# A sixth token group with 16 instead of 12 row pairs in seven products, and LN2 transposes that wait for both tiles' stores

## The chip, the cores and the metric

One core of one Trainium2 chip. The metric is the time of one execution on the device, in microseconds (us), as the median of several executions. Engines: PE is TensorE, ACT is ScalarE, DVE is VectorE, POOL is GpSimd, SP is SyncE, which issues nearly all DMAs. LN2 is the layer norm ahead of the MLP.

## The reference, cut to what matters

```
h  = x + A(layernorm(x))                 # sliding, dilated attention, S = 2048, D = 576, 32 heads; ends in @ wo
h2 = h + gelu(layernorm(h) @ w1 + b1) @ w2 + b2        # F = 4608
```

## The kernel before

Tokens are worked in 8 groups of two tiles of 128. Each group goes through MLP1 (324 matmuls), and then through MLP2, in the middle of which stands Wo, the attention's output product, for the *next* group. MLP2 sums over F = 36 blocks of 128, taken as 18 row pairs. A pair is a 2x2 block product and may be done with 7 matmuls (products P1 to P7) in place of 8, if DVE first makes sums of the h blocks and of the w2 blocks. From the third group on some of the 18 pairs are done so: 8, 12, 12, 12, 18 and 18.

The order of one MLP2 with 12 pairs, and what its words do (cut):

```
ROWS = {2: 8, 3: 12, 4: 12, 5: 12, 6: NM, 7: NM}                  # k = 5 is the sixth group; NM = 18
steps = [(1, all_), "b", "wo", "h", "e", (2, all_), "11", (6, all_), "d", "6", "7", (7, all_), "rest", "in",
         (5, all_), "f", "exp", (4, all_), "21", "22", "o1", "4", (3, all_), "12", "o0", "3"]
# (n, rows): product n on PE.   "11" "12" "21" "22": the rows that are left plain, on PE.
# "b", "d", "f": ACT copies one PSUM bank into another, which the next product adds to:
seed = {"b": (1, 6), "d": (6, 5), "f": (5, 3)}                    # "d" copies P6's bank into P5's
nc.scalar.copy(out=bank[seed[step][1]], in_=bank[seed[step][0]])
# "h": LN2's statistics and the last sums;  "6", "7": ACT scales tile c, tile d, and SP stores them;
# "in": the two DMA transposes of these stores, which the next MLP1 reads (hnT)
...
def dma_out(src):                                                 # a tile is stored by two DMAs, 144 KB and 16 KB
    td = dram.tile([P, KT * P], BF16, tag="td", name="td", bufs=4)
    nc.sync.dma_start(out=td[:, 0:D], in_=src)
    nc.sync.dma_start(out=td[:, D:KT * P], in_=src[:, KF * P:D])
    return td

def ln2_in(j):
    read[0] = nc.sync.dma_start_transpose(out=hnT_slot(j), in_=hn.pop(j)[:]).ins
```

The instructions of an engine run in the order in which this code issues them. In what follows c and d are the first and the second tile of the next group.

## Time and profile before

| | before |
|---|---|
| time, median (lowest to highest) | 365.13 (364.87 to 365.61), 3 runs |
| PE busy, matmuls | 359.0 us of 363.3, 4899 |
| sixth group, first MLP2 matmul to the next group's first MLP1 matmul | 272.10 to 290.79 = 18.69 us |

The last row is the piece that the change is about. It is read from the timeline of PE, and it has 168 matmuls and no gap. The lines behind these numbers are in the prediction; one more on which it rests is c's second store of the sixth group's input, held up while an instruction fetch was under way:

```profile
246.03 1.92 SPq L192 DMA_DIRECT2D td<-hn  x1
```

### The profile page before, as it was taken

The page shows a single profiled execution, that of the slowest core. Times are in us where ns is not written, and L with a number is a line of the kernel's source. Part 1 is how long each engine was busy: PE and PEld are TensorE (multiplying, and loading weights), DVE is VectorE, ACT ScalarE, POOL GpSimd, SP SyncE. Part 2 cuts the span into 40 slices and gives each one's busy share as a digit, 9 for nine tenths or more (in the row PEclk, how much of TensorE's full clock was granted, in tenths as well). Part 3 has the DMA queues.
Part 4 walks back from the last instruction along what each step waited for, and adds up shares of the span by engine and source line. Part 5 has one row for each costly group of instructions (what it writes and reads, how often), then busy time and mean ns, then how long its engine had stood idle before and what let it go on. Part 6 is the DMA issues. An engine that isn't in the chain of part 4 may idle for free.

```text
span 363.3 us, 11427 instructions
## 1 busy us (share of the span) xinstructions
PE 359.0 (99%) x4899; PEld 292.3 (80%) x4899; DVE 299.1 (82%) x422; ACT 229.3 (63%) x507; POOL 39.4 (11%) x47
## 2 busy tenths in 40 slices
PE   8999999999999999999999999999999999999996
PEld 5688977888788877887788778877987788778874
DVE  5999999999899999999999899979994599720431
ACT  4779856799527763668456855685568556615630
POOL 2251004000120030103100211020101010100000
PEclk9999999999999999999999999999999999999999
DMA  7979999965455833711652156304530442030001
GB/s 235 321 187 294 231 261 233 366 217 80 144 101 96 194 134 87 153 39 35 143 99 71 35 134 108 70 32 106 121 70 33 90 86 56 3 90 18 2 2 33
DMA packets 61907, 43.70 MB, mean 120 GB/s; under 512 B 31888, under 2 KB 60176, under 8 KB 61856
## 3 DMA queue, kind: packets, MB, share of 16 engines
q1 hardware_dynamic: 59968, 41.13, 43.2%
q0 software_dynamic: 1728, 1.77, 4.6%
q8 instruction: 38, 0.62, 0.7%
q10 hardware_dynamic: 160, 0.07, 0.1%
q14 instruction: 13, 0.11, 0.1%
HBM read 21.10 MB, written 12.42 MB: 92 GB/s over the span
## 4 chain that ended last, share of the span: by engine, by line
PE 98%; DMA 1%; DVE 0%; ACT 0%; SPq 0%; issue 0%
PE pm L215 39%; PE po L659 27%; PE pq L215 15%; PE po L574 10%; PE pw L215 5%; PE xt_pt L182 1%; DMA x_all<-in_A_x_dram 1%; PE xt_pt L186 0%; ACT q_all L810 0%; PE h_pt L182 0%; PE o_pt L182 0%; DVE o_sb L690 0%; SPq L104 0%; DVE q_all L789 0%; PE h_pt L186 0%; PE o_pt L186 0%
## 5 line engine op out<-in xcount | busy, mean ns | idle before, releaser
L555 ACT ACTIVATE h_all<-pm,b_sb 128x256 f16<-128x256 f32 (+1 forms) x288 | 108.5, 497 | 76.7 <-PE pm L215 76.7
L215 PE MATMUL pm<-hnT,w_sb 64*128 64x256 bf16 x2304 | 143.0, 269 | 0.0
L215 PEld LDWEIGHTS <-w_sb 64*128 64x128 bf16 x2304 | 112.0, 94 | 14.7 <-issue 1.7
L659 PEld LDWEIGHTS <-h_all 128*128 128x128 f16 x544 | 52.3, 98 | 15.3 <-issue 2.5
L215 PE MATMUL pq<-wq_sb,xnT 64*128 64x288 bf16 x768 | 54.4, 283 | 0.0
L215 PEld LDWEIGHTS <-xnT 64*128 64x128 bf16 x864 | 42.8, 94 | 9.8 <-DMA xnT<-xd 0.2
L349 DVE TENSOR_TENSOR prod<-prod 128x2304 bf16<-128x2304 bf16 (+1 forms) x64 | 44.2, 691 | 2.1
L659 PE MATMUL po<-w2a_sb,h_all 128*128 128x288 bf16 (+1 forms) x312 | 43.6, 286 | 0.0
L395 DVE TENSOR_TENSOR prod<-kv_ring,probs 128x4608 bf16<-128x4608 bf16 x16 | 40.9, 2555 | 0.4
L343 DVE TENSOR_TENSOR prod<-kv_ring,q_all 128x4608 bf16<-128x4608 bf16 x16 | 40.8, 2549 | 0.2
L215 PE MATMUL pm<-hnT,w1h_sb 64*128 64x256 bf16 x288 | 39.3, 269 | 0.0
L401 DVE TENSOR_TENSOR prod<-prod 128x2304 bf16<-128x2304 bf16 (+1 forms) x32 | 33.8, 1057 | 1.0
L574 PEld LDWEIGHTS <-h_all 128*128 128x128 bf16 x288 | 27.9, 98 | 7.9 <-issue 0.9
L479 POOL TENSOR_TENSOR ln_rstd<-ln_var,mhalf 128x1 f32<-128x1 f32 x13 | 14.4, 1108 | 174.7 <-ACT ln_var L478 174.7
L574 PE MATMUL po<-w2a_sb,h_all 128*128 128x288 bf16 x224 | 28.5, 286 | 0.0
L659 PEld LDWEIGHTS <-kv_ring 128*128 128x128 f16 x240 | 23.5, 98 | 5.9
L659 PE MATMUL po<-w2b_sb,h_all 128*128 128x288 bf16 (+1 forms) x152 | 22.2, 286 | 0.0
L639 DVE TENSOR_TENSOR kv_ring<-h_all 128x1536 f16<-128x1536 f16 (+3 forms) x10 | 6.9, 686 | 16.0 <-ACT h_all L555 16.0
L215 PE MATMUL pw<-wo_sb,oT 64*128 64x288 bf16 x256 | 19.5, 283 | 0.0
L162 POOL TENSOR_TENSOR ln_rstd<-ln_veps,mhalf 128x1 f32<-128x1 f32 (+2 forms) x14 | 13.4, 962 | 47.9 <-DVE ln_veps L156 31.6
L215 PEld LDWEIGHTS <-oT 64*128 64x128 bf16 x288 | 13.5, 94 | 4.8 <-issue 1.7
L503 POOL DMA_DIRECT2D x_all<-h x12 | 10.9, 1060 | 54.6 <-DMA x_all<-in_A_x_dram 25.0
(107 smaller groups left out, 375.9 us busy)
## 6 DMA issues: line engine op xcount, KB each, us to landing
w_sb<-in_B_w_dram SPq DMA_DIRECT2D x6, 768.0 KB, 6.1
kv_ring<-kv_dram SPq DMA_DIRECT2D x28, 144.0 KB, 2.7
w2a_sb<-in_B_w_dram SPq DMA_DIRECT2D x4, 1008.0 KB, 6.3
kv_dram<-kv_ring SPq DMA_DIRECT2D x13, 288.0 KB, 4.6
out_dram<-o_sb SPq DMA_DIRECT2D x15, 144.0 KB, 2.7
td<-q_all SPq DMA_DIRECT2D x14, 144.0 KB, 2.5
td<-hn SPq DMA_DIRECT2D x14, 144.0 KB, 1.8
x_all<-in_A_x_dram SPq DMA_DIRECT2D x12, 144.0 KB, 3.0
```

What stands on the lines that cost most here:

```text
L162: nc.gpsimd.tensor_tensor(out=rstd[:], in0=veps[:], in1=mhalf[:].to_broadcast([P, n]), op=ALU.pow)
L215: last = nc.tensor.matmul(duo["g"][r ^ swap][i], lhsT=lhsT, rhs=rhs, start=(swap == 0 and i == 0 and kt == 0), stop=(swap == 1 and kt == K ...
L343: nc.vector.tensor_tensor(out=prod[:], in0=k_ring[j % 2], in1=q_all[:, j, :].unsqueeze(1) .to_broadcast([P, W, D]), op=ALU.mult)
L349: nc.vector.tensor_tensor(out=prod[:, :, o * H:o * H + n], in0=prod[:, :, a * H:a * H + n], in1=prod[:, :, c * H:c * H + n], op=ALU.add)
L395: nc.vector.tensor_tensor(out=prod[:].rearrange("p w (d h) -> p w d h", h=H), in0=v_ring[j % 2].rearrange("p w (d h) -> p w d h", h=H), in ...
L401: nc.vector.tensor_tensor(out=prod[:, 0:n, :], in0=prod[:, 0:n, :], in1=prod[:, n:2 * n, :], op=ALU.add)
L479: nc.gpsimd.tensor_tensor(out=rstd[:], in0=var[:], in1=mhalf[:], op=ALU.pow)
L503: ins = nc.gpsimd.dma_start(out=x_of(j), in_=h_of.pop(j)[:], accum_op=ALU.add).ins
L555: pace[0] = nc.scalar.activation(out=hT(grp)[:, f, 0:N], in_=ps[:, r, i * N:(i + 1) * N], func=ACT.Gelu_apprx_tanh, bias=b1_sb[:, f:f + 1] ...
L574: nc.tensor.matmul(banks[half], lhsT=hT(grp)[:, f, i * P:(i + 1) * P], rhs=w2_rows(f)[:, half * HALF:(half + 1) * HALF], start=(f == 0), s ...
L639: nc.vector.tensor_tensor(out=s_slot(t, m0, m1), in0=a, in1=b, op=alu)
L659: nc.tensor.matmul(bank, lhsT=l, rhs=r, start=start, stop=stop, skip_group_check=True)
```

## The change

Four row pairs more of the sixth group go through the seven products: four matmuls fewer. The sums for them come late on DVE, so the first 12 rows of P6 and P7 go ahead of the last 4 of each. Besides, at every group the first LN2 transpose waits until tile d's last store has landed, so that no LN2 store is in flight beside an LN2 transpose. Cut to its core:

```diff
     def dma_out(src):
...
-        nc.sync.dma_start(out=td[:, D:KT * P], in_=src[:, KF * P:D])
+        stored[0] = nc.sync.dma_start(out=td[:, D:KT * P], in_=src[:, KF * P:D]).ins
...
     def ln2_in(j):
         read[0] = nc.sync.dma_start_transpose(out=hnT_slot(j), in_=hn.pop(j)[:]).ins
+        if stored[0] is not None:
+            tc.add_manual_dep(read[0], stored[0].name, sync_dep, reason="stores ahead of the transposes of LN2")
+            stored[0] = None
...
+        if SR < rows < NM:                                        # SR = 12
+            steps = [(1, all_), "b", "wo", "h", "e", (2, all_), "11", (6, lo), (7, lo), "6", "7", (6, hi), "d", (7, hi), "rest", "in",
+                     (5, all_), "f", "exp", (4, all_), "21", "22", "o1", "4", (3, all_), "12", "o0", "3"]
...
-        ROWS = {2: 8, 3: 12, 4: 12, 5: 12, 6: NM, 7: NM}
+        ROWS = {2: 8, 3: 12, 4: 12, 5: 16, 6: NM, 7: NM}
...
+                if k == 5:
+                    m1[1] += [c_(w2_sums, 12, 14)]
+                    x["h"] += [c_(h_sums, SR, rows), c_(w2_sums, 14, 16)]
...
-                    m1[1] = [c_(w2_sums, *m) for m in ((12, 14), (14, 16), (16, NM))]
+                    ring1_free[0] = True
+                    m1[1] = [c_(w2_sums, 16, NM)]
```

(Cut: the rows of q_all in which the new sums and "rest" are kept, and that only the first 12 rows' sums are called where all were.)

More of the change, by code (lines that the diff above doesn't have):

```diff
@@ L186, in transpose_in @@
         nc.tensor.transpose(pt[0:HP, KF, :], src[:, KF * P:D], ident[:])
+    stored = [None]
     def dma_out(src):
@@ L609 @@
     SR = 12
+    ring1_free = [False]
     RING_T = 3 * SR * P
@@ L617, in s_slot @@
             return ring_blocks(0, (i * SR + m0) * P, m1 - m0, P)
+        if not ring1_free[0]:
+            return q_all[:, 11 - 2 * i, (m0 - SR) * P:(m1 - SR) * P].bitcast(F16).rearrange("p (m c) -> p m c", c=P)
         return ring_blocks(1, 6 * HALF + (i * (NM - SR) + m0 - SR) * P, m1 - m0, P)
@@ L685, in mlp2_fast @@
         flat = kv_ring[int(rows == NM)][:].rearrange("p w t d -> p (w t d)")
-        rest = halves(flat[:, W * 2 * D - 2 * D:W * 2 * D].bitcast(F32))
+        rest = q_all[:, 13:16:2, :].bitcast(F32) if SR < rows < NM else halves(flat[:, W * 2 * D - 2 * D:W * 2 * D].bitcast(F32))
         bank = {1: a, 2: a, 3: f, 4: b, 6: b}
@@ L705, in take @@
             bank[7], bank[5] = (psum_pair(tag, "po")[:, 0, 0:HALF] for tag in (r, s))
-        lo, hi, all_ = (0, min(rows, SR)), (SR, rows), (0, rows)
+        lo, hi, all_ = (0, SR), (SR, rows), (0, rows)
         seed = {"b": (1, 6), "d": (6, 5), "f": (5, 3)}
@@ L714, in mlp2_fast @@
         }
-        if rows <= SR:
+        if SR < rows < NM:
+            steps = [(1, all_), "b", "wo", "h", "e", (2, all_), "11", (6, lo), (7, lo), "6", "7", (6, hi), "d", (7, hi), "rest", "in",
+                     (5, all_), "f", "exp", (4, all_), "21", "22", "o1", "4", (3, all_), "12", "o0", "3"]
+        elif rows <= SR:
             steps = [(1, all_), "b", "wo", "h", "e", (2, all_), "11", (6, all_), "d", "6", "7", (7, all_), "rest", "in",
@@ L1015 @@
                 early = {2: (), 3: (0,)}.get(k, (0, 2))
-                m1[3] += [c_(h_sums, 0, rows, early)]
-                x["h"] += [c_(h_sums, 0, rows, [t for t in range(4) if t not in early])]
+                m1[3] += [c_(h_sums, 0, min(rows, SR), early)]
+                x["h"] += [c_(h_sums, 0, min(rows, SR), [t for t in range(4) if t not in early])]
+                if k == 5:
+                    m1[1] += [c_(w2_sums, 12, 14)]
+                    x["h"] += [c_(h_sums, SR, rows), c_(w2_sums, 14, 16)]
                 x["exp"] += [c_(exps, e, f), c_(att_den, e, f)]
```

## The prediction

> **What bounds the kernel now.** I read the page's busy line first, then the chain that ended last in order of time, then the timelines of PE, ACT, DVE and the DMA issues around the sixth group.
>
> ```profile
> PE 359.0 (99%) x4899; PEld 292.3 (80%) x4899; DVE 299.1 (82%) x422; ACT 229.3 (63%) x507; POOL 39.4 (11%) x47
> PE 98%; DMA 1%; DVE 0%; ACT 0%; SPq 0%; issue 0%
> ```
>
> TensorE is 99% busy and 98% of the chain, so time can only come from fewer matmuls, and every nanosecond in which PE is made to wait is paid in full. The chain shows the sixth group (MLP1, first product, Wo, the rest of MLP2) and the same end of the seventh:
>
> ```profile
> 254.37 17.79 PE pm L215 x324
> 272.17 1.58 PE po L659 x12
> 273.74 2.31 PE pw L215 x36
> 276.06 14.81 PE po L659 x120
> ...
> 312.54 14.07 PE po L659 x114
> ```
>
> A row pair in seven products takes 7 matmuls, one left plain takes 8. With 12 of 18 pairs in products that is 12x7 + 6x8 = 132 (12 + 120 here), with all 18 it is 126 (12 + 114). There is no gap between the pieces: before the change PE waits for nothing in this stretch. So the question is only what the change removes and what new wait it makes.
>
> **What the Trainium skill says.** "TensorE: Matmul & The Clock Gate", section "Back-to-back issue gap", gives a warm gap of N/2.4 + 2.5 ns, 122.5 ns for 288 columns. The trace agrees: twelve matmuls of P6 run from 278.94 to 280.41, 122.5 ns each (the 286 ns on the page is latency, not spacing). "ScalarE: Activation LUTs", section "What ACT_TABLE_LOAD costs", says that back-to-back ACTIVATEs overlap by about 93 ns; the trace has hn d's scale starting at 282.006 where the one before ends at 282.099, also 93 ns. "DMA: Bandwidth & Descriptors", section "Two DMAs through the same engine are not ordered", says the order a kernel has is the completion semaphore; each transpose here waits for its own tile's stores already, so the new wait is for timing, not for correctness. "Runtime: NRT & Kernel Launch", section "Instruction fetch mechanics", says instructions come in 16 KiB blocks by DMA; the page has 38 such packets on queue 8, one of them at 246.2 and one at 284.8, both just when a group's LN2 result is stored.
>
> **The change part by part.** In what follows c and d are the two tiles of the next group.
>
> *Removed.* Four matmuls, 4 x 122.5 ns = 0.49 us, all on the path.
>
> *DVE in the sixth group.* The built order shows that w2 sums of rows 12-14 come ahead of the early h sums, and h sums of rows 12-16 plus w2 sums of rows 14-16 come between the last h sums and "rest".
>
> ```profile
> 271.48 0.95 DVE L639 TENSOR_TENSOR kv_ring<-h_all 128x1536 f16<-128x1536 f16 x1
> 272.46 0.96 DVE L639 TENSOR_TENSOR h_all<-h_all 128x1536 f16<-128x1536 f16 x1
> 275.61 1.42 DVE L459 TENSOR_TENSOR h<-pw,x_all 128x576 f32<-128x576 f32 x2 [2.18 <-PE pw L215]
> 276.95 0.95 DVE L639 TENSOR_TENSOR kv_ring<-kv_ring,h_all 128x1536 f16<-128x1536 f16 x1
> 277.93 0.96 DVE L639 TENSOR_TENSOR kv_ring<-h_all,kv_ring 128x1536 f16<-128x1536 f16 x1
> 282.08 0.76 DVE L690 TENSOR_TENSOR kv_ring<-po,x_all 128x576 f32<-128x576 f32 x1 [3.19 <-PE po L659]
> ```
>
> The seventh group has the same operations: four w2 sums of two rows take 1.72 us (299.87 to 301.59), four h sums of four rows about 1.5 us. The first four fit into the idle 2.18 us ahead of L459; so that one still starts on PE's word, 0.49 us later (276.10), because P1 now has 16 rows ahead of Wo. Then h sums to 279.38, the new h sums to 280.86, the new w2 sums to 282.58. PE needs the last of them (for P7, row 14) at about 282.62. Just in time: 0 to 0.1 us.
>
> *The ACT order, the step that decides.* Before, the copy that seeds P5's bank ("d") stood right behind P6, with P7 to hide it, and the two LN2 sends came after it. Now it stands behind the second half of P6, and the sends (hooks "6" and "7") are ahead of it in ACT's order.
>
> ```profile
> 280.00 0.29 ACT L478 ACTIVATE ln_var<-ln_var,eps 128x1 f32<-128x1 f32 x1
> 280.61 0.38 ACT L728 COPY po<-po 128x288 f32<-128x288 f32 x1 [0.31 <-PE po L659]
> 280.90 0.30 ACT L484 ACTIVATE ln_nmean<-ln_nmean,ln_rstd 128x1 f32<-128x1 f32 x1
> 281.23 0.87 ACT L175 ACTIVATE hn<-h,ln_nmean,ln_rstd 128x576 bf16<-128x576 f32 x1
> 282.01 0.28 ACT L484 ACTIVATE ln_nmean<-ln_nmean,ln_rstd 128x1 f32<-128x1 f32 x1
> 282.32 0.87 ACT L175 ACTIVATE hn<-h,ln_nmean,ln_rstd 128x576 bf16<-128x576 f32 x1
> ```
>
> LN2's statistics end at 280.30 + 0.49 = 280.79 (they hang on Wo's end). The sends take 280.90 to 283.19 = 2.28 us, so to 283.10. The copy starts 0.09 before that and takes 0.38: to 283.40, and PE sees it at about 283.43. PE by itself: P2 starts at 275.99 + 0.49 = 276.48, P6's first rows after 20 matmuls (P2 16, plain 4) at 278.93, P7's first 12 at 280.40, P6's last 4 at 281.87, P7's last 4 at 282.36, P5 at 282.85. It waits 283.43 - 282.85 = 0.58 us. This eats the whole saving: -0.49 + 0.58 = +0.09. Even without the sends the copy could not end before 282.36 + 0.16 (the last matmul's latency beyond its slot) + 0.04 + 0.38 = 282.94, 0.09 late.
>
> *Buffers.* The upper sums and "rest" move to rows of q_all whose queries and outputs are done with; their waits in the built order are on stores issued a whole group earlier, so they cost nothing.
>
> *Later in the group.* exp follows the copy "f" and moves by some 2 us, and with it the denominators and the last output sum (292.12 to about 294.2). Its bank is needed by the seventh group's second visit at about 294.8: 0.6 us of slack, so nothing. DVE has eight sums fewer in the seventh group; PE waits there for nothing today, so that is worth nothing.
>
> *The transposes, all groups.* The first transpose of a pair now also waits for d's last store. The second is issued 1.3 us behind the first, and MLP1 needs both.
>
> ```profile
> 248.00 0.43 SPq L191 DMA_DIRECT2D td<-hn  x1
> 248.47 0.43 SPq L192 DMA_DIRECT2D td<-hn  x1
> 249.00 0.41 SPq L340 DMA_DIRECT2D kv_ring<-kv_dram  x1
> 249.58 2.54 SPq L494 DMA_TRANSPOSE hnT<-td  x2
> ```
>
> The trace puts the landing of d's last store at 250.01, so this pair moves from 249.58 to about 250.06, by 0.48. The second transpose was issued at 250.90 and landed 3.27 later, at 254.17; the wait on it on PE's queue ended at 254.20 and the first MLP1 matmul of the sixth group came at 254.31, some 0.1 later than the spacing allows. This pair has no slack at all. It is so late because the fetch at 246.2 held up c's store (its issue took 1.92 us), and PE's stream up to there does not change, so the fetch will fall there again. Moved by 0.48, with a landing that may be 0.0 to 0.24 shorter (3.03 in the third group, which has the same reload behind it), PE loses 0.25 to 0.48; I take 0.40. Elsewhere there is slack: the delays are 0.5 (fourth and fifth groups' inputs), 1.0 and 1.3 us (last and first two), against 0.9 to 2.4 us between landing and use. For the seventh group the wait helps: before, d's last store, issued at 283.58, landed only at 287.39, behind c's transpose, and d's transpose at 290.31, 0.5 us ahead of its use. It should land at 289.4 to 290.1. That is safety, not time, because PE did not wait there.
>
> Sum: 365.13 - 0.49 + 0.58 + 0.40 = 365.62.
>
> **The rivals.** *The saving comes through whole (364.6).* For it: PE is the bound, the matmuls really go, and splitting P6 and P7 was meant to hide the sums. Against it: ACT's order as built, with numbers above; it would need the sends to be over 0.58 us earlier, and they hang on PE's own Wo. *The new wait on stores speeds transposes up enough to pay for itself (365.2).* For it: stores and a transpose in flight together are slow in the sixth group (2.46 us of issue instead of 1.21). Against it: the other pairs take the normal 1.21 us with a store in flight, and where a wait is already hidden (all pairs but the sixth group's input) a faster transpose buys nothing. *The DVE becomes the bound (366 or more).* The sums of rows 14-16 end within 0.1 us of their use, and a POOL power that takes 1.3 us (as in the fifth group) instead of 0.55 would move the second send and the seed copy by up to 0.35 more. For it: no slack; against it: the copy wait already covers the first of these.
>
> **Range and chances.** The wait on the copy is fairly sure (0.4 to 0.9), the one on the transposes less (0 to 0.5), the saving is sure. Best case -0.49 + 0.1 + 0, worst -0.49 + 0.95 + 0.6; runs of one kernel spread by 0.7. I say 365.6, range 364.7 to 366.2. 2% is 7.3 us, far beyond any of these terms.
>
> **What would show it.** In the changed profile: 128 + 36 matmuls of MLP2 and Wo in group six; an idle of about 0.6 us on PE at the first matmul of P5, released by ACT's copy at L739, which starts right behind the second LN2 scale; about 0.4 us of PE at the sixth group's first MLP1 matmul, ended by a landing of hnT; no such idle at the other groups; d's last store of the seventh group landing within 2 us. If PE shows no idle at P5, my reading of ACT's order is wrong and the time is near 365.0; if there is none at either, 364.6.

## The result, and the profile after

| | before | after |
|---|---|---|
| time, median (lowest to highest), 6 runs each | 365.12 (364.87 to 365.69) | 365.20 (364.80 to 365.29) |
| PE busy, matmuls | 359.0, 4899 | 357.6, 4895 |
| the sixth group's piece | 18.69 | 272.13 to 290.78 = 18.65 |

The ratio is 0.9998, 95% interval 0.9985 to 1.0011: the same. (A ratio here is the mean time of one kernel's fast runs over that of the other's of the same rounds, so not quite the ratio of the medians.) Four matmuls are gone and the time is not. From the page of the changed kernel, busy line and engines' shares of the chain that ended last:

```profile
PE 357.6 (98%) x4895; PEld 290.5 (80%) x4895; DVE 300.6 (83%) x426; ACT 228.9 (63%) x507; POOL 39.4 (11%) x47
PE 94%; DMA 2%; ACT 1%; SPq 1%; DVE 0%; issue 0%
```

PE's share of the chain fell from 98% to 94%: somewhere the chain now leaves PE. The same chain in order of time (start, length, what) says where:

```profile
254.41 17.79 PE pm L217 x324
272.20 2.07 PE po L667 x16
...
282.12 0.87 ACT hn L175
282.99 0.30 ACT po L739
283.30 0.04 issue
283.34 7.51 PE po L667 x60
290.85 17.79 PE pm L217 x324
```

It goes through ACT's scaling of tile d (hn) and the seed copy "d" (po L739) before it comes back to PE at P5. The share alone overstates this: a chain that goes back over the engine which waited last leaves out all that PE did meanwhile. What was lost is read from the timeline of PE, where the bracket has the idle time and what ended it:

```profile
281.91 0.65 PE L667 MATMUL po<-q_all 128*128 128x288 f16 x4
282.40 0.41 PE L667 MATMUL po<-w2a_sb,h_all 128*128 128x288 f16 x2
282.65 0.41 PE L667 MATMUL po<-w2b_sb,h_all 128*128 128x288 f16 x2
283.34 1.63 PE L667 MATMUL po<-x_all,kv_ring 128*128 128x288 f16 x12 [0.29 <-ACT po L739]
```

The last four rows of P6, then of P7, then P5. The bracket's 0.29 counts from the modelled end of P7's last matmul. From start to start it is 571 ns where 122.5 is usual, so the loss is 0.45 us, against 4 x 122.5 ns = 0.49 saved: 0.04 is left, which is 18.69 - 18.65. ACT, the same stretch:

```profile
282.12 0.87 ACT L175 ACTIVATE hn<-h,ln_nmean,ln_rstd 128x576 bf16<-128x576 f32 x1
282.90 0.39 ACT L739 COPY po<-po 128x288 f32<-128x288 f32 x1
```

P6 was done at 282.28 + 0.29 = 282.57 (last of its four starts at 282.28, 286 ns of latency). The copy starts at 282.90 with no idle ahead of it: it stood in line behind the scaling. DVE, which makes the sums, was done with the last of them in time for P7's row 14 at 282.65:

```profile
282.14 0.45 DVE L637 TENSOR_TENSOR w2b_sb<-w2b_sb 128x576 f16<-128x576 bf16 x1
```

Last, the transposes of the sixth group's input among the DMA issues of SP, where I had expected 0.40 us of loss:

```profile
246.07 1.22 SPq L194 DMA_DIRECT2D td<-hn  x1
...
247.80 0.43 SPq L194 DMA_DIRECT2D td<-hn  x1
...
249.42 2.53 SPq L496 DMA_TRANSPOSE hnT<-td  x2
```

The store behind the instruction fetch was held for 1.22 us and not for 1.92, so d's store was issued 0.67 earlier (247.80 against 248.47), and the transposes, in spite of their new wait, 0.16 earlier than before (249.42 against 249.58). The second landed at 253.66, by the trace's landing record, 2.93 after its issue (3.27 before), and PE's first matmul on it came at 254.34.

### The profile page after: what moved, and what is told of

The parts are those of the page before. It is cut to its first block, busy times and chain, and to the rows that moved or that the text cites. A ratio compares the mean times of both kernels' runs of the same rounds, so it can differ in the third digit from the quotient of the medians.

```text
span 363.3 us, 11427 instructions
## 1 busy us (share of the span) xinstructions
PE 357.6 (98%) x4895; PEld 290.5 (80%) x4895; DVE 300.6 (83%) x426; ACT 228.9 (63%) x507; POOL 39.4 (11%) x47
## 4 chain that ended last, share of the span: by engine, by line
PE 94%; DMA 2%; ACT 1%; SPq 1%; DVE 0%; issue 0%
PE pm L217 39%; PE po L667 25%; PE pq L217 14%; PE po L579 10%; PE pw L217 5%; DMA wq_sb<-in_A_wqkv_dram 1%; SPq L104 1%; PE xt_pt L182 1%; DMA x_all<-b_bc 1%; ACT hn L175 0%; ACT hn L479 0%; PE h_pt L182 0%; PE o_pt L182 0%; DVE h L461 0%; ACT hn L478 0%
## 5 line engine op out<-in xcount | busy, mean ns | idle before, releaser
L667 PEld LDWEIGHTS <-h_all 128*128 128x128 f16 x528 | 50.8, 98 | 14.9 <-issue 2.5
L667 PE MATMUL po<-w2a_sb,h_all 128*128 128x288 bf16 (+1 forms) x302 | 42.0, 286 | 0.0
L667 PE MATMUL po<-w2b_sb,h_all 128*128 128x288 bf16 (+1 forms) x142 | 21.2, 286 | 0.0
L739 ACT COPY po<-po 128x288 f32<-128x288 f32 x18 | 6.9, 384 | 16.2 <-PE po L667 13.0
```

Source lines behind the costliest of these rows:

```text
L667: nc.tensor.matmul(bank, lhsT=l, rhs=r, start=start, stop=stop, skip_group_check=True)
```

## The experiments

Theory A: the four matmuls save 0.49 us, and the seed copy behind the LN2 sends gives 0.45 back; the wait on the stores costs nothing. Rivals are that the wait on the stores costs something that the rows earn (B), or that it is what lets the rows earn anything (C). A fourth theory, D, came out of the second run. All runs computed the reference's result. "Wait" in this table is the idle of PE in the profile of that run, beyond the spacing usual at that place; "piece" is the sixth group's.

| run | median | before, same chip | ratio, 95% interval | piece | wait at P5 | other waits from the sixth group on |
|---|---|---|---|---|---|---|
| e1 | 365.26 | 365.15 | 1.0000 (0.9988 to 1.0012) | 18.65 | 0.44 | none |
| e2 | 366.56 | 365.15 | 1.0035 (1.0017 to 1.0053) | 18.70 | 0 | eighth group 0.82 |
| e3 | 364.96 | 365.15 | 0.9997 (0.9984 to 1.0009) | 18.43 | 0.22 | none |
| e4 | 366.75 | 365.15 | 1.0056 (1.0032 to 1.0080) | 19.48 | 0 | seventh group 1.28 |
| e5 | 366.26 | 365.49 | 1.0011 (0.9975 to 1.0048) | 18.70 | 0 | sixth group 0.19 |
| e6 | 366.03 | 365.49 | 1.0004 (0.9967 to 1.0042) | 18.65 | 0.44 | eighth group 1.02 |
| e7 | 364.99 | 365.49 | 0.9977 (0.9939 to 1.0015) | 18.20 | 0 | none |
| e8 | 365.04 | 365.49 | 0.9976 (0.9933 to 1.0019) | 18.20 | 0 | none |
| e9 | 365.24 | 365.24 | 0.9999 (0.9987 to 1.0012) | 18.69 | 0 | none |
| e10 | 365.94 | 365.24 | 1.0019 (1.0006 to 1.0031) | 18.69 | 0 | eighth group 0.98 |
| e11 | 364.84 | 365.24 | 0.9989 (0.9975 to 1.0002) | 18.20 | 0 | none |
| e12 | 365.28 | 365.24 | 0.9998 (0.9984 to 1.0012) | 18.65 | 0.44 | none |

Totals of single executions wander, because the first stages do: the second group's MLP1 starts anywhere from 106.55 to 107.65 us in these profiles. The piece is the same to 0.01 us in every profile of the same order of instructions. So the waits are judged by the profiles, the totals only by intervals. On the chip of e5 to e8 two runs of the kernel before took 369.42 and 370.48 us, both at a granted clock of 0.995. The second counts as slow and is left out; the first does not, and it widens those intervals and makes the kernel before look 0.4 us slower. The mean of the nine others is 365.40, against 366.27, 366.01, 365.02 and 365.00 for e5 to e8.

**e1, the rows alone**

```diff
     def ln2_in(j):
         read[0] = nc.sync.dma_start_transpose(out=hnT_slot(j), in_=hn.pop(j)[:]).ins
-        if stored[0] is not None:
-            tc.add_manual_dep(read[0], stored[0].name, sync_dep, reason="stores ahead of the transposes of LN2")
-            stored[0] = None
```

> The changed kernel without the wait of the transposes on both tiles' stores: 16 row pairs alone. Theory A (the four matmuls save 0.49 us and the wait of P5 for ACT's seed copy gives back 0.45; the new wait on the stores costs nothing): about 365.2 us, the same 0.4 to 0.5 us of PE idle at P5, and the piece from the first product of the sixth group to the next MLP1 is 18.6 to 18.7 us as in the changed kernel. The last store of tile d in the seventh group's input is again held behind tile c's transpose (landing 2 to 4 us after issue). Theory B (rows gain 0.4 net and the wait on the stores costs it again): 364.8 us. Theory C (the wait on the stores is what keeps the seventh group's transposes in time): a PE wait at the seventh group's first MLP1 matmul, 365.3 to 366.

Measured: 365.26 us, the piece 18.65, P5 waits as in the changed kernel, nothing else waits. As A has it; B and C fall. One detail of A was wrong: d's store was not held behind c's transpose this time (the second transpose landed at 288.69 where the kernel before had 290.31). That hold is not in every execution.

**e2, the wait on the stores alone** (the three lines of e1 and the `stored` variable, added to the kernel before)

> The kernel before with only the wait of the LN2 transposes on both tiles' stores. Theory A: 365.1 us, no PE wait anywhere that the kernel before does not have, transposes issued 0.4 to 1.3 us later in each group. Theory B, which is the 0.40 term of my prediction: 365.4 to 365.6 us with a PE wait of 0.25 to 0.48 us at the sixth group's first MLP1 matmul, if the instruction fetch holds the first tile's store for as long as it did in the profile of before.

Measured: 366.56 us, 0.35% *slower*, and surely so. Not at the sixth group: no wait there. PE waits 0.82 us at the eighth group's first MLP1 matmul, for the second transpose, which took 4.85 us from issue to landing, where the same profile has 2.8 to 2.9 at the other groups. The chain there:

```profile
323.24 4.85 DMA hnT<-td
328.09 0.14 issue
328.23 17.86 PE pm L217 x324
```

(Its profile lost another 0.87 us before the second group's MLP1, 107.49 against 106.62; e3 did so too, without harm to its piece, and no run says why.) So theory A is wrong in one point: the wait on the stores is not free by itself, and yet it is in the changed kernel. The packets in the trace showed what was different: a 16 KiB instruction fetch lies from 326.005 to 326.927, and of the 1280 packets of 256 bytes that the two transposes move the last five begin at 326.913 and after, the one ahead of them at 325.991. The profiles of e6 and e10 have the same picture, with five packets that wait for the end of the fetch's. Theory D: the wait on the stores moves this transpose by 1.0 us into the fetch, and in the changed kernel the four matmuls fewer (8 instructions with their weight loads) move the fetch out of its way.

**e3, the seed copy on DVE**

```diff
-                nc.scalar.copy(out=bank[seed[step][1]], in_=bank[seed[step][0]])
+                copy = nc.vector.tensor_copy if step == "d" and SR < rows < NM else nc.scalar.copy
+                copy(out=bank[seed[step][1]], in_=bank[seed[step][0]])
```

> The changed kernel with the seed copy of P5's bank in the sixth group on VectorE instead of ScalarE, so that it need not stand behind the two LN2 sends. Theory A: P6's last matmul ends near 282.56 in the changed kernel, DVE is free at 282.59, a copy of 288 from PSUM takes about 0.45, so P5 starts near 283.09 and not 283.34: PE idle at P5 0.2 us instead of 0.45, time 0.25 us shorter than the changed kernel, 364.95. Rival (the wait at P5 is for DVE's late sums or for something else that the profile puts down to ACT): idle unchanged, 365.2.

Measured: DVE makes the copy as soon as its last sum and P6 are done, and PE follows at its end. Timeline of DVE, then of PE (this profile stands 1.1 us later here than that of the changed kernel: 0.9 was lost before the second group, 0.2 in the third):

```profile
283.22 0.45 DVE L637 TENSOR_TENSOR w2b_sb<-w2b_sb 128x576 f16<-128x576 bf16 x1
283.67 0.47 DVE L740 COPY po<-po 128x288 f32<-128x288 f32 x1
```

```profile
283.73 0.41 PE L667 MATMUL po<-w2b_sb,h_all 128*128 128x288 f16 x2
284.19 0.65 PE L667 MATMUL po<-x_all,kv_ring 128*128 128x288 f16 x4
```

345 ns from start to start: 0.22 of wait, where 0.20 was expected, and a piece of 18.43. This is the run that shows the cause at P5: nothing changed but the engine of one copy, and half of the wait went. The total (364.96) moved as expected, within its noise.

**e4, two sums earlier, P6 and P7 whole, in the old order**

```diff
-            steps = [... "11", (6, lo), (7, lo), "6", "7", (6, hi), "d", (7, hi), "rest", "in",
+            steps = [... "11", (6, all_), "d", "6", "7", (7, all_), "rest", "in",
...
-                    x["h"] += [c_(h_sums, SR, rows), c_(w2_sums, 14, 16)]
+                    m1[3] += [c_(w2_sums, 14, 16, (0, 1))]
+                    x["h"] += [c_(h_sums, SR, rows), c_(w2_sums, 14, 16, (3, 2))]
```

> The changed kernel with two of the w2 sums of rows 14-16 (those that P6 and P5 need) moved ahead into DVE's idle before the sums for LN2, and the old order of products: P6 whole, seed copy, sends, P7 whole. Theory A: the copy ends near 281.5 while P7 runs to 282.9, so no PE idle at P5 and the sixth group's MLP2 with Wo takes 18.2 us; 364.75 us, unless the LN2 sends, 0.4 us later, make the seventh group's transposes land after 290.3, which would give back up to 0.3. Rival (DVE's sums bind): PE idle inside P6 or P7, no gain.

Measured: no wait at P5, as A has it, and 1.28 us of wait at the seventh group instead, four times what I had allowed. The DMA issues of SP, and then the chain:

```profile
284.18 0.44 SPq L194 DMA_DIRECT2D td<-hn  x1
287.33 2.54 SPq L496 DMA_TRANSPOSE hnT<-td  x2
```

```profile
288.64 2.90 DMA hnT<-td
291.55 0.14 issue
291.68 17.86 PE pm L217 x324
```

With the copy ahead of the sends, d's last store was issued at 284.18 instead of 283.39 in the changed kernel. That put it in flight when the fetch came (285.20 to 286.08): the last 8 of its 128 packets begin at 286.07, it landed after 3.1 us, at 287.26, instead of 1.5, and the transposes wait for it. So the order of the change, sends ahead of the copy, has a reason; it pays 0.45 at P5 to keep the stores early. And A holds: 19.48 - 1.28 = 18.20, the whole 0.49.

**e5 and e6, the fetch moved by the warm-up.** Before the work PE does 13 warm-up matmuls. Taking 4 away or adding 4 shifts every later fetch by 8 instructions against the work.

```diff
-        for n in [512] * 8 + [P] * 5:          # e5: e2 with this
+        for n in [512] * 8 + [P]:
```

```diff
-        for n in [512] * 8 + [P] * 5:          # e6: the changed kernel with this
+        for n in [512] * 8 + [P] * 9:
```

> The kernel before with the wait on both tiles' stores, as in e2, but with 4 of the 13 warm-up matmuls taken away at the very start, so that every later 16 KiB instruction fetch of PE falls 8 instructions (0.5 us) later in the work, as it does in the changed kernel from the sixth group on. Theory D (in e2 the eighth group's second transpose meets an instruction fetch and its last packets wait for it; the four matmuls fewer of the changed kernel move the fetch behind the transpose): 365.0 to 365.3 us and no wait at the eighth group's first MLP1 matmul, the fetch starting after the transpose's last packets. Rival (the wait on the stores costs 1 us by itself, through the later transposes alone): 366.3 to 366.7 as in e2.

> The changed kernel with 4 more warm-up matmuls at the start (they end about 0.1 us after PE is needed), so that the fetches of the last groups fall as in e2. Theory D: a wait of about 1 us at the eighth group's first MLP1 matmul in most executions, 366.0 to 366.6 us. Rival (the fetch has nothing to do with it): 365.2 to 365.4 us as the changed kernel.

Measured, e6: 366.03 us, where the changed kernel had 365.20, and 1.02 us of wait at the eighth group. Its chain there:

```profile
322.27 5.05 DMA hnT<-td
327.32 0.14 issue
327.45 17.86 PE pm L217 x324
```

Four matmuls more in the first 5.3 us, and a transpose 317 us later takes 5.05 us. Measured, e5: the wait at the eighth group is gone, as D has it. The total is a miss: 366.26 us against 365.0 to 365.3. In its profile 1.03 us were already lost before the second group's MLP1 (107.65 against 106.62), and 0.19 at the sixth group, for its second transpose. Whether the missing warm-up costs the first microsecond I did not test; e2 and e3 lost 0.87 and 0.93 there with all of the warm-up.

All profiles at the eighth group, from the packet records, in us from the moment when PE would have begun its MLP1 (its last MLP2 matmul plus 0.218):

| runs | wait on stores there | PE instructions | second transpose issued | fetch begins | transpose's last packet ends | PE waits |
|---|---|---|---|---|---|---|
| before, e9 | no | as before | -5.20, -5.21 | -2.40, -2.73 | -2.58, -2.81 | 0 |
| e1, e8 | no | 8 fewer | -5.21, -5.21 | -1.17, -1.27 | -2.79, -2.80 | 0 |
| e2, e10 | yes | as before | -4.17, -4.16 | -1.40, -1.25 | -0.31, -0.15 | 0.82, 0.98 |
| e6 | yes | as before, by warm-up | -4.16 | -1.20 | -0.10 | 1.02 |
| after, e3, e12 | yes | 8 fewer | -4.17, -4.16, -4.15 | -0.19, -0.25, -0.15 | -1.65, -1.70, -1.68 | 0 |
| e5 | yes | 8 fewer, by warm-up | -4.16 | -0.25 | -1.71 | 0 |
| e4, e7, e11 | yes | 8 fewer | -4.17, -4.16, -4.16 | 0.57, 0.17, 0.57 | -1.76, -1.70, -1.70 | 0 |

In the three runs with the wait at this group and the old count, the fetch comes just ahead of the last packets and the transpose ends 1.3 to 1.7 us later than in the other runs with the wait; in no other run. Two things stay open. One is why the fetch begins 1.0 to 2.0 us later for 8 instructions that are worth 0.49 us of matmuls. The other is that the fetch does not stand still while the transpose is moved: at the same count it begins 1.0 to 1.5 us later with the wait on the stores than without it (-1.40 and -1.25 against -2.40 and -2.73). That the fetch holds the last packets is shown; why it falls where it does is not.

**e7 and e8, for the whole saving.** As e4, but the copy on DVE between the sums, so that ACT's sends stay early; e8 without the wait on the stores.

```diff
# e7: e4 and e3 together, and
-                    x["h"] += [c_(h_sums, SR, rows), c_(w2_sums, 14, 16, (3, 2))]
+                    x["h"] += [c_(h_sums, SR, rows)]
+                    x["6"] += [c_(w2_sums, 14, 16, (3, 2))]
```

> e4 with the seed copy on VectorE between the sums, so that the LN2 sends on ScalarE stay where they are in the changed kernel. Theory A: copy at 281.1 to 281.55, P7 runs to 282.9, no PE idle at P5, MLP2 with Wo of the sixth group 18.2 us, LN2 sends end at 283.0 and the seventh group's transposes land by 290.0 as in the changed kernel: 364.75 us. If the transposes meet the fetch at 285 as in e4, a wait at the seventh group's first MLP1 matmul and 365 to 366.

> e7 without the wait of the transposes on both tiles' stores. Theory A: the same 0.49 us saved in the sixth group, 364.7 us, and the seventh group's transposes either land as early as in e1 (288.7) or, when a fetch holds tile d's last store behind tile c's transpose as in the kernel before, at about 290.3, which is where PE needs them: at most 0.1 us of wait. If the wait on the stores is needed for the gain: a wait of over 0.3 us there, 365.1 or more.

Measured: 18.20 us for the piece in both, no wait anywhere from the sixth group on; 364.99 and 365.04 us. The wait on the stores is not needed for the gain. The chip was noisy, so e7 ran again as e11.

**e9 and e10, the wait on the stores split**

```diff
-        if stored[0] is not None:                                     # e2
+        if stored[0] is not None and j not in GROUPS[-1]:             # e9
+        if stored[0] is not None and j in GROUPS[-1]:                 # e10
```

> The kernel before with the wait on both tiles' stores at every group's input except the eighth's. Theory D (what e2 lost was lost at the eighth group alone, where the delayed transpose meets the fetch): 365.1 to 365.4 us, no wait at the eighth group's first MLP1 matmul. Rival (the wait costs at several groups, as at the sixth in my prediction): 365.5 to 366.5 us.

> The kernel before with the wait on both tiles' stores at the eighth group's input only. Theory D: most of e2's loss, 0.8 to 1.2 us of wait at the eighth group's first MLP1 matmul in most executions, 365.9 to 366.4 us, the second transpose's last packets after the fetch. Rival: 365.1 to 365.3 us.

Measured: e9 365.24, as the kernel before on that chip; e10 365.94, 0.19% slower, all five runs above all nine of the kernel before. e2's loss sits at the eighth group, as D has it, though e2's median lost more (1.4 against 0.7 us; 0.87 of what its profile lost was lost before the second group). The profile of e10 puts its wait down to DVE's output sum, which ended 0.1 us before PE went on; but the kernel before has the same sum at the same time (326.65 to 327.41) and PE began at 326.55 without it. The last packets of the transpose, at 326.4, are 2.4 us later than in the kernel before.

**e11 and e12, the best and the changed kernel in the same rounds** (no edit to e7 and to the changed kernel)

> The kernel of e7 again, on a chip with the changed kernel beside it. Theory A: no PE wait from the sixth group on, 364.65 us, 0.45 to 0.55 below the kernel before and the changed kernel. Rival: the gain of e7 was that chip's noise, ratio 1.000.

> The changed kernel again, in the same rounds as e11. Theory A: 365.1 to 365.2 us, PE idle at P5 0.45 us, no other wait; the profile also shows whether the fetch at the eighth group again starts after the transpose's last packets.

Measured: 364.84 and 365.28 us. The chain of e11 runs through the sixth group on PE alone:

```profile
272.41 2.07 PE po L667 x16
274.48 2.31 PE pw L217 x36
276.79 13.83 PE po L667 x112
290.62 17.79 PE pm L217 x324
```

16 + 112 matmuls of MLP2 without a gap. The order of e11 does beat both kernels in this piece, by 0.49 and 0.45 us in each of the three profiles that have it. As a total, 0.11% below the kernel before, its interval (0.9975 to 1.0002) just touches 1: likely, but not shown by the times alone.

## Why the prediction was right or wrong

The time (365.62 predicted, 365.20 measured) lies in the stated range, but that range is 1.5 us wide and would have held no change as well as a loss. The forecast itself, a kernel slower by 0.49 us, lies just outside the measured interval (+0.40 us at most). What can be judged is the mechanism. Of its three terms one was exact, one right in kind and too large, and one was not there.

1. *The saving, -0.49.* Right: e4 (less its wait at the seventh group), e7, e8 and e11, which have no wait at P5, show 18.20 against 18.69. The section "Back-to-back issue gap", which the prediction cites for the 122.5 ns, gives that formula for an isolated matmul and says that in a stream of weight loads and matmuls it counts too little at small N and too much at large N; that this stream keeps to it at 288 columns is the trace's word, not the page's.
2. *The copy behind the sends, +0.58.* The mechanism is as predicted, and e3 shows it by moving the copy. The size was 0.45. LN2's statistics ended at 280.82 (280.79 predicted); but the first send did not start after them at 280.82, it overlapped them by 0.09, and so the copy ended at 283.29 and not at 283.40; P5 could have begun at 282.89 and not at 282.85. Not all of the 0.45 is due to the sends: with only four matmuls of P7 left to hide it, the copy would by the prediction's estimate be 0.09 late even without them, and no run separates the two. (A slip of reading without effect: what starts at 282.006 in the kernel before is not tile d's scaling but the small instruction ahead of it, L484; the overlap of 0.093 is as told.)
3. *DVE just in time.* Right: the last sum ended at 282.59, 282.58 predicted.
4. *The transposes, +0.40.* This is the step that failed. "This pair has no slack at all" was so in the profile of before, though not for the reason given. The 0.22 us between the last MLP2 matmul and the first of MLP1, taken for a wait of 0.1, is no wait: the same 0.218 stands at every group's boundary. But the second transpose landed 0.135 us ahead of that matmul, and 0.135 is also what lies between the two where PE does wait (e4 at the seventh group, e5 at this one). What failed is the step from there to a cost: that the fetch "will fall there again" and hold the store as long, and that the landing could be at most 0.24 shorter. In the changed kernel the hold was 1.22 us in place of 1.92 and the landing took 2.93 in place of 3.27. And e11 has nearly the same hold, with the wait on the stores:

```profile
246.28 1.80 SPq L194 DMA_DIRECT2D td<-hn  x1
...
250.21 2.54 SPq L496 DMA_TRANSPOSE hnT<-td  x2
```

   There the pair was issued 0.39 later, seen from PE's first matmul at 254.55, but the second landed 0.37 sooner after its issue (2.90), again 0.135 ahead of PE, and PE waits for nothing. Of the ten profiles with the wait at this group nine show no idle there, and e5 shows 0.19. The 3.27 was one sample as the hold was: e1, e8 and e10, without the wait, have 2.90 to 3.00.
5. *"Elsewhere there is slack."* True of the changed kernel, and wrong as an argument: I compared the delay with the slack (1.0 at the eighth group, against 0.9 to 2.4) and did not ask what the delayed transpose would meet. In e2, e6 and e10 it meets a fetch and lands some 2 us later.
6. *For the seventh group the wait is safety.* The second transpose landed at 289.87, within the 289.4 to 290.1 predicted. e1 and e8 had no need of it.

So the expected gain went where step 2 says: into a wait for a copy that the new order puts behind the sends. The wait on the stores is free in this kernel only because the fetch at the eighth group comes later with four matmuls fewer: e6, which puts the 8 instructions back ahead of the work, pays 1.02 us.

## What to carry to other kernels

When work is reordered on the engine that bounds, follow each small helper instruction on the other engines to its new place in their order: here a copy of 0.39 us, put behind two sends, took back the gain of four matmuls, and another engine had room for it. Before delaying a DMA on the ground that it has slack, look at what else uses the DMA engines at its new time, instruction fetches too; here 8 instructions more or fewer moved one by 1.0 us and more. Judge a change of 0.1% by pieces of the profile that repeat to 0.01 us, and take a hold or a landing time seen in one profile as one sample.

## What the Trainium skill lacked or had wrong

- "Runtime: NRT & Kernel Launch", section "Instruction fetch mechanics": it calls the cost of crossing a 16 KiB boundary mostly hidden. No gap of PE stands at a fetch itself here (e11 runs through four of them from 254.62 to 290.62), but the fetch packet lasts 0.88 to 1.48 us in the profile of before and can hold the kernel's own DMAs: a transpose of 4.85 and 5.05 us in place of 2.8 to 2.9 (e2, e6), a 16 KB store of 3.1 in place of 1.5 (e4).
- "DMA: Bandwidth & Descriptors", section "Queues, rings and completion order", has "refill" in row 14. The pages of these profiles put the 38 instruction packets of 16 KiB on queue 8, and only 13 or 14 smaller ones on queue 14. Whether the profile's queue numbers are the rows is not shown.
- No page that I read gives a time for the change from a matmul stream of 128 rows to pairs of 64 rows, though "TensorEngine Tiling (Array Packing)", section "Key Properties", says that changing the tiling mode drains TensorE. From start to start it is 0.218 us at all boundaries from MLP2 to MLP1, against 0.1225 within the stream. It is easily taken for a wait.
- "ScalarE: Activation LUTs", section "What ACT_TABLE_LOAD costs", has the overlap of back-to-back ACTIVATEs alone. The seed copy, a COPY, too began 0.09 us before the end of the instruction ahead of it (282.900 against 282.992).
